# A two-level Strassen kernel: all attention chunks first, and x operands that stay in SBUF

## The chip, the cores and the metric

The kernel runs on one core of a Trainium2 chip. A core has TensorE (PE: matrix products, with the weight load shown apart as PEld), VectorE (DVE), ScalarE (ACT), GpSimd (POOL), SyncE (SP, which here issues nearly all DMAs) and 16 DMA engines; each engine runs its own instruction stream in order. The metric is the device time of one execution in microseconds (us), lower is better. Before the change it is 1186.68 us, the median of three runs (1186.55 to 1187.57).

## The reference

Two blocks follow each other. The first is a decayed linear attention with batch B=4, H=8 heads, S=768 positions and head width D=64; the second sends its output, seen as x of 3072 tokens by 512 features, through four experts.

```python
# attention, block by block along the sequence
intra = einsum('bhic,bhjc->bhij', qb, kb) * Dmask
intra = einsum('bhij,bhjd->bhid', intra, vb)
inter = einsum('bhid,bhde->bhie', qb * lam_pow, kv_state)
out[:, :, sl] = intra + inter
kv_state = lam_block * kv_state + einsum('bhsd,bhse->bhde', kb * rev_pow, vb)
# experts, E=4, DM=512, F=1024
p = domain_probs / (domain_probs.sum(-1, keepdims=True) + 1e-09)
for e in range(E):
    h = maximum(x @ w1[e], 0.0)
    out += p[:, e:e+1] * (h @ w2[e])
```

All data is fp32.

## The kernel before, in words

**Attention.** The work is cut into 24 chunks of 128 positions, six to a batch. A chunk has three pieces. `turn` transposes q and k on TensorE against an identity (L529), eight transposes, copies both from PSUM with ScalarE (L534, L535), scales q on VectorE (`qs`), and lets GpSimd multiply k by its decay (`decayed`). `scores` makes the key-query products into two PSUM banks (L551), and VectorE multiplies them by the decay mask into two tiles `st`. `values` reads the state (L574), multiplies masks and values (L579), and makes the next state's share (L587) in the unused half of one of its two banks; ScalarE copies the output (L592) into `xT`, and VectorE updates `kv`. In batches 2 and 3, from the third chunk on, q and k come in another way: `bring_across` lays them out again in DRAM in small pieces, and `turn_across` transposes 32 by 32 blocks on VectorE, so that TensorE has no transposes for these eight chunks.

**The experts.** Tokens are taken in three groups of 1024 (eight chunks), experts one after the other: units (g, e), 12 in all. Each unit has a first product x @ w1 and a second h @ w2. Both are written with Strassen's scheme in the Winograd form: seven outer products M1 to M7 of sums of quarters. The first product is split a second time: each outer M has seven inner products of two matmuls of 128 x 128 by 128 x 256 (`first_product`, L843), for which the seven inner operands of x and of w1 are loaded from DRAM, 896 KB each (`feed`). Evacuation is an add on VectorE (`tt`, recorded at L95), or a ScalarE copy (L851). The last group's second product is nested too (`nested_product`, L1123), with the last results turned at the end.

Operands are prepared on GpSimd: `prepare_w1`, `prepare_w2` and `prepare_x` form the quarter sums and inner sums and store them to DRAM (`w1_ops`, `w2_sums`, `x_ops`). They are lists of small steps called chores. `pump` issues them by a clock of slots `now`, an estimate `busy` of GpSimd's work (one slot for each 480 elements a partition), and puts a store two slots behind its work. `until` forces chores out where a load needs them. VectorE sums that may be delayed stand in the list `background`, from which `rest` takes one at a time; `soon` puts new items at its front.

**The order.** The first group's eight chunks are written out in ten iterations: iteration i has turn i, scores i-1 and values i-2, with three pairs of PSUM banks used in turn (`pairs[n % 3]`), so that turn i+1 takes the pair of values i-2. From iteration 4 quarters of unit (0,0)'s first products stand between the pieces. That unit alone uses one Strassen level (`direct_product`, L1253): each outer product is 16 matmuls from plain quarters of w1. The operands of unit (0,1) are formed on the fly (`own_x`, `own_w1`) and stored for later. From then on a loop runs over the units: it interleaves the second product of one unit with the first product of the next, seven steps of eight slots, and places one attention piece of the next group now and then in a slot.

`load` issues q, k and v of a chunk on SP as rows of 64 numbers. The pool of 128 x 512 tiles (`small`) has `NPOOL` = 47 buffers; `stream` has two buffers each for x and w1 operands.

Of the kernel before, what the change touches and what calls it, by code (L numbers as in the profile page):

```python
# [11 lines left out]
AF = mybir.ActivationFunctionType  # L12
# [5 lines left out]
NPOOL = 47  # L18
AHEAD = 2
# [3 lines left out]
def kernel(  # L23
# [11 lines left out]

# [22 lines left out]
    stream = ctx.enter_context(tc.tile_pool(name="stream", bufs=2))  # L76
    opool = ctx.enter_context(tc.tile_pool(name="o", bufs=CPG))
# [4 lines left out]

# [25 lines left out]

    nat = {}

    def load(n, names="qkv"):

        b, c = divmod(n, NCH)
        for name in names:
            x = small(f"{name}n")
# [12 lines left out]
    x_ops = dram.tile([NG, 7, P, 7, 256], FP32, name="x_ops")  # L128
# [4 lines left out]
    X_AT = {n: i for i, n in enumerate(("M1", "M7", "M6", "M4", "M5", "M2", "M3"))}  # L133


# [58 lines left out]

    def inner_x(eng, g, m, blk):
        at = {"B11": (0, 0), "B12": (0, 1), "B21": (1, 0), "B22": (1, 1)}
        inner(eng, ("x", g, m), x_ops[g, MS.index(m)], blk, T_OPS, at)
# [103 lines left out]
    xT = consts.tile([P, 4, G], FP32, name="xT")  # L301

    b11, b21 = xT[:, 0:2, 0:W], xT[:, 2:4, 0:W]
    b12, b22 = xT[:, 0:2, W:G], xT[:, 2:4, W:G]

    def prepare_x(g):

        st = {}

        def total(name, a, b, op):  # L310
            t = stage.tile([P, 2, W], FP32, name="xo", tag="st")
            halves(t[:], a, b, op)
            st[name] = t[:]

        def ready(m, blk):
            inner_x(nc.gpsimd, g, m, blk)

        return [lambda: ready("M1", b11), lambda: ready("M2", b21)], [
            lambda: total("T1", b12, b11, ALU.subtract), lambda: ready("M5", st["T1"]),
            lambda: total("T2", b22, st["T1"], ALU.subtract), lambda: ready("M6", st["T2"]),  # L320
            lambda: total("T3", b22, b12, ALU.subtract), lambda: ready("M7", st["T3"]),
            lambda: ready("M3", b22),
            lambda: total("T4", b21, st["T2"], ALU.subtract), lambda: ready("M4", st["T4"]),
        ]


# [3 lines left out]
    w1_now = {0: {}, 1: {}}  # L330

    def raw_w1(e, name):
        i, j = int(name[1]) - 1, int(name[2]) - 1
        if name in ("A21", "A22"):
            to = tuple(small("w1b")[:] for _ in range(2))
        else:
            t = stage.tile([P, 2, W], FP32, name="w1b", tag="st")
            to = t[:, 0], t[:, 1]
# [1179 lines left out]
```

## Time and profile before

| what | value |
|---|---|
| median of three runs | 1186.68 us |
| span of the profiled execution, first to last instruction | 1183.3 us |
| what lies around the span, median less span | 3.4 us |
| PE busy | 1175.7 us (99%), 6559 instructions |
| DVE busy | 790.7 us (67%) |
| POOL busy | 628.7 us (53%) |
| ACT busy | 274.0 us (23%) |
| moved by DMA | 324.23 MB, mean 274 GB/s |
| x operand loads | 70 of 896 KB, 6.4 us from issue to landing |
| w1 operand loads | 70 of 896 KB, 8.7 us from issue to landing |

The profile is of one execution; no total time of its own is given for it beyond the span, so the 3.4 us are the difference to the median of the runs. Busy shares are averages over the stages: the opening (attention of the first group with the first unit's direct products, up to about 90 us), the steady stage up to about 690 us, the last group with its nested second products, and the end. Matmuls overlap, each shown with its whole latency of 380 ns or so; how fast TensorE goes is read from the distance between their starts. A line such as L95 is a helper: the tiles' names tell the operations apart.

### The profile page before, as it was taken

The page shows a single profiled execution, that of the slowest core. Times are in us where ns is not written, and L with a number is a line of the kernel's source. Part 1 is how long each engine was busy: PE and PEld are TensorE (multiplying, and loading weights), DVE is VectorE, ACT ScalarE, POOL GpSimd, SP SyncE. Part 2 cuts the span into 40 slices and gives each one's busy share as a digit, 9 for nine tenths or more (in the row PEclk, how much of TensorE's full clock was granted, in tenths as well). Part 3 has the DMA queues.
Part 4 walks back from the last instruction along what each step waited for, and adds up shares of the span by engine and source line. Part 5 has one row for each costly group of instructions (what it writes and reads, how often), then busy time and mean ns, then how long its engine had stood idle before and what let it go on. Part 6 is the DMA issues. An engine that isn't in the chain of part 4 may idle for free.

```text
span 1183.3 us, 17880 instructions
## 1 busy us (share of the span) xinstructions
PE 1175.7 (99%) x6559; PEld 1022.7 (86%) x6559; DVE 790.7 (67%) x1333; ACT 274.0 (23%) x500; POOL 628.7 (53%) x600
## 2 busy tenths in 40 slices
PE   9999999999999999999999999999999999999998
PEld 8888888888888888888888888888888888888887
DVE  6785785567468857647856774773665676777785
ACT  3332122112211201211220120121243342341331
POOL 2756258349457900055244655416584693783884
PEclk9999999999999999999999999999999999999999
DMA  9797799999999997899998989998986657566543
GB/s 232 194 292 238 250 300 310 362 326 333 353 359 334 328 291 227 262 287 303 303 317 247 295 287 318 275 312 294 316 289 238 261 196 272 212 237 248 213 155 95
DMA packets 265608, 324.23 MB, mean 274 GB/s; under 512 B 121489, under 2 KB 206897, under 8 KB 265521
## 3 DMA queue, kind: packets, MB, share of 16 engines
q1 hardware_dynamic: 254912, 320.27, 81.6%
q10 hardware_dynamic: 10608, 2.82, 1.1%
q8 instruction: 52, 0.85, 0.3%
q14 instruction: 36, 0.29, 0.1%
HBM read 237.69 MB, written 89.54 MB: 277 GB/s over the span
## 4 chain that ended last, share of the span: by engine, by line
PE 94%; DVE 3%; DMA 2%; issue 0%; POOL 0%; SPq 0%; ACT 0%; DVEq 0%
PE pg L843 38%; PE q L897 32%; PE pq L1123 13%; PE pM L1253 2%; PE op L579 2%; PE sp L551 2%; PE pc L1253 2%; DMA w_ops<-ops 2%; PE op L574 1%; PE op L587 1%; DVE sums L95 0%; PE qp L529 0%; PE kp L529 0%; PE pg L1123 0%; DVE acc L95 0%; DVE m L95 0%
## 5 line engine op out<-in xcount | busy, mean ns | idle before, releaser
L843 PE MATMUL pg<-xs_in,ws_in 128*128 128x256 f32 x1960 | 469.8, 380 | 0.9 <-DVE m L95 0.9
L843 PEld LDWEIGHTS pg<-xs_in,ws_in 128*128 128x128 f32 x1960 | 371.2, 190 | 52.9 <-DVE m L95 2.3
L95 DVE TENSOR_TENSOR m<-pg,m 128x512 f32<-128x512 f32 x451 | 308.1, 687 | 106.5 <-PE pg L843 99.6
L897 PE MATMUL q<-w2t,hS 128*128 128x256 f32 x1024 | 243.4, 380 | 0.0
L897 PEld LDWEIGHTS q<-w2t,hS 128*128 128x128 f32 x1024 | 193.2, 190 | 27.0 <-issue 0.2
L913 DVE SCALAR_TENSOR_TENSOR acc<-q,gate,acc 128x256 f32<-128x256 f32 x192 | 92.5, 482 | 170.2 <-PE q L897 170.0
L897 PE MATMUL q<-w2t,m 128*128 128x256 f32 x768 | 182.7, 381 | 0.0
L897 PEld LDWEIGHTS q<-w2t,m 128*128 128x128 f32 x768 | 144.8, 190 | 20.5 <-issue 0.3
L855 ACT ACTIVATE m<-m 128x512 f32<-128x512 f32 x132 | 83.0, 630 | 283.6 <-DVE m L95 276.6
L95 POOL TENSOR_TENSOR m<-m,xT 128x512 f32<-128x512 f32 x64 | 80.7, 1276 | 71.6 <-ACT m L855 53.9
L95 POOL TENSOR_TENSOR kn<-kn,s_decay 128x512 f32<-128x512 f32 x20 | 22.5, 1126 | 140.7 <-PE kp L529 134.8
L95 DVE TENSOR_TENSOR sums<-pq,sums 128x256 f32<-128x256 f32 x153 | 64.2, 422 | 46.0 <-PE pq L1123 38.8
L851 ACT COPY m<-pg 128x512 f32<-128x512 f32 x88 | 51.6, 586 | 174.3 <-PE pg L843 173.4
L1123 PE MATMUL pq<-acc,w2t 128*128 128x256 f32 x352 | 86.6, 379 | 0.0
L95 POOL TENSOR_TENSOR ops<-w2b 128x256 f32<-128x256 f32 x24 | 17.9, 766 | 119.4 <-DMA w2b<-in_moe_w_dram 111.3
L1123 PEld LDWEIGHTS pq<-acc,w2t 128*128 128x128 f32 x352 | 66.8, 190 | 9.3 <-issue 0.3
L95 POOL TENSOR_TENSOR acc<-hT,hT 128x512 f32<-128x512 f32 x32 | 40.3, 1274 | 30.3 <-PE pq L1123 28.4
L95 POOL TENSOR_TENSOR w2o<-w2b 128x512 f32<-128x512 f32 x32 | 40.6, 1291 | 23.3 <-DMA w2b<-in_moe_w_dram 23.3
L786 ACT ACTIVATE m<-m 128x512 f32<-128x512 f32 x44 | 27.7, 630 | 101.8 <-DVE m L95 101.8
L95 DVE TENSOR_TENSOR hS<-m,m 128x512 f32<-128x512 f32 x56 | 45.3, 812 | 4.9 <-ACT m L855 4.9
L95 DVE TENSOR_TENSOR m<-m,m 128x512 f32<-128x512 f32 x56 | 47.2, 844 | 0.0
L95 POOL TENSOR_TENSOR acc<-hT,acc 128x512 f32<-128x512 f32 x32 | 40.7, 1273 | 7.4 <-PE pq L1123 5.4
(158 smaller groups left out, 1360.4 us busy)
## 6 DMA issues: line engine op xcount, KB each, us to landing
xs_in<-x_ops SPq DMA_DIRECT2D x70, 896.0 KB, 6.4
ws_in<-w_ops SPq DMA_DIRECT2D x70, 896.0 KB, 8.7
w2t<-w_ops SPq DMA_DIRECT2D x66, 256.0 KB, 6.8
w2t<-w_sums SPq DMA_DIRECT2D x64, 256.0 KB, 3.9
w_ops<-ops SPq DMA_DIRECT2D x28, 512.0 KB, 5.5
w2t<-in_moe_w_dram SPq DMA_DIRECT2D x48, 256.0 KB, 3.4
w2b<-in_moe_w_dram SPq DMA_DIRECT2D x32, 256.0 KB, 5.9
w_sums<-w2o SPq DMA_DIRECT2D x16, 512.0 KB, 5.1
```

The source lines that it names most:

```text
L95: eng.tensor_tensor(out=o, in0=a, in1=b, op=op)
L551: nc.tensor.matmul(out=sp[r][:, ac * C:(ac + 1) * C], lhsT=hc(kT)[half[r], ac], rhs=hc(qT)[half[r], ac], start=True, stop=True,)
L574: nc.tensor.matmul(out=op[r][half[x], a * C:(a + 1) * C], lhsT=kv[half[r], 2 * a + x], rhs=hc(qs)[half[r], 2 * a + x], start=(a == 0), sto ...
L579: nc.tensor.matmul(out=op[r][half[x], a * C:(a + 1) * C], lhsT=vn[:, 4 * r + 2 * a + x], rhs=hc(st[r])[:, 2 * a + x], start=(first and a = ...
L786: nc.scalar.activation(out=o[:], in_=o[:], func=AF.Relu)
L843: nc.tensor.matmul(out=p[:, j * 256:(j + 1) * 256], lhsT=ws[i][:, j * P:(j + 1) * P], rhs=xs[i], start=(fresh and j == 0), stop=True, skip ...
L851: nc.scalar.copy(out=new[at][:], in_=p[:])
L855: nc.scalar.activation(out=new[at][:], in_=new[at][:], func=AF.Relu)
L897: nc.tensor.matmul(out=p[:, s * DH:(s + 1) * DH], lhsT=h[A_OF[m]][:, c * 256 + s * P:c * 256 + (s + 1) * P], rhs=fed2[g, e, m][uu][:, c], ...
L913: nc.vector.scalar_tensor_tensor(out=o, in0=x, scalar=w, in1=o, op0=ALU.mult, op1=ALU.add)
L1123: nc.tensor.matmul(out=p[:, 0:256], lhsT=fed3[e, m, x // 2][:, x % 2, c * P:(c + 1) * P], rhs=b[B_OF[i]][:, c * 256:(c + 1) * 256], start= ...
L1253: nc.tensor.matmul(out=p[:, s * 256:(s + 1) * 256], lhsT=a[c][:, f:f + P], rhs=b[:, c, j * 256:(j + 1) * 256], start=(s == 0 and c == 0 an ...
```

## The change

- All 24 attention chunks stand at the start. Iterations 0 to 13 of the same three-piece pattern run with nothing between (`DENSE = 14`); scores come ahead of turn in iteration 3 alone. The remaining 33 pieces are spread over the first 35 slots of unit (0,0)'s first product, at a rate of `len(attention) / 35` a slot.
- All chunks are turned on TensorE; `bring_across`, `turn_across` and what belongs to them go.
- Unit (0,0) takes `first_product` with two Strassen levels like all others, with w1 operands formed on the fly in the stream buffers (`own_fill`, `own_inner`), and stored for later groups. `direct_product`, `own_x`, `own_w1` and the one-level sums go. Unit (0,1) reads its w1 operands from DRAM, as prepared by `prepare_w1(1)`.
- Seven tiles `xs` (pool `xp`, one buffer each) hold all inner operands of a group's x for its four units. Group 0's are written directly: values copies the plain quarters a second time, VectorE makes the quarter sums (`pair_sums`, chunks 4 to 7), and `x_inner` makes the inner sums, M1's and M2's on VectorE, the others on GpSimd.
- For groups 1 and 2, plain quarters and GpSimd's pair sums are stored in `x_blocks` (128 KB a piece), and `x_fill` brings 512 KB a block into a slot while the last unit of the group before runs; GpSimd then makes the inner sums. The stores and the 896 KB loads of `x_ops` are gone.
- While the dense part lasts, delayed VectorE work is issued at once; afterwards it goes through the front of `background`, and values forces what it needs (`settle_up`).
- `NPOOL` is 37; k and v are loaded into the buffers of `acc` and `w2`. The w2 operands of the last unit go to the seven x slots.

```diff
-NPOOL = 47
-AHEAD = 2
+NPOOL = 37
+DENSE = 14
...
+    xp = ctx.enter_context(tc.tile_pool(name="xp", bufs=1))
...
+    def x_inner(g, m, eng):
+        t = slots[g, m]
+        for o, x, y in ((4, 3, 1), (1, 1, 0), (5, 3, 1), (6, 2, 5)):
+            tt(eng, t[:, o], t[:, x], t[:, y], ALU.subtract)
+        made.add(("x", g, m))
+
+    def x_fill(g, m):
+        t = slot(g, m)
+        nc.sync.dma_start(out=whole(t), in_=x_blocks[g - 1, MS.index(m)])
+        chores.insert(0, lambda: x_inner(g, m, nc.gpsimd))
...
+        work = [once(f) for f in work]
+        owed[what] = work
+        if dense[0]:
+            settle_up(what)
+        else:
+            background[0:0] = work
...
     def values(n, tags):
+        settle_up(("qs", n), ("st", n), ("kv", n - 1))
...
+            nc.scalar.copy(out=x[:, r * 256:(r + 1) * 256], in_=op[r][:, 0:256])
+            if r in plain and g == 0:
+                nc.scalar.copy(
+                    out=whole(slots[0, plain[r]])[:, :, at], in_=op[r][:, 0:256].rearrange("p (a t) -> p a t", t=C),
+                )
...
+            for t, a, b in (("T1", b12, b11), ("T2", b22, o["T1"]), ("T3", b22, b12), ("T4", b21, o["T2"])):
+                tt(nc.vector if g == 0 else nc.gpsimd, o[t], a, b, ALU.subtract)
...
+    attention = [
+        (i, f, i - lag) for i in range(NT + 2)
+        for f, lag in (((scores, 1), (turn, 0), (values, 2)) if i == 3 else ((turn, 0), (scores, 1), (values, 2)))
+        if 0 <= i - lag < NT
+    ]
+
+    def attend():
+        i, f, n = attention.pop(0)
+        f(n, pairs[n % 3])
+        if not attention or attention[0][0] != i:
+            if i + 4 < NT:
+                load(i + 4, "qk")
+            if 4 <= i + 3 < NT:
+                load(i + 3, "v")
+        return i
...
+    chores.extend((
+        lambda: (own_fill("M1"), raw_w1("A21", "A22")), pause(4),
+        lambda: own_inner("M1"), lambda: own_sum("S1"), lambda: (own_fill("M5"), raw_w1("A11")),
+        lambda: own_inner("M5"), lambda: own_sum("S2"),
+        *prepare_w2(0),
+    ))
+    for i in range(DENSE):
+        while attention[0][0] == i:
+            at_turn = attention[0][1] is turn
+            attend()
...
+    rate = len(attention) / 35
+    for i, m in enumerate(SEQ):
...
+        for f in first_product(0, 0, m, blocks, ("g1", "g3")):
+            f()
+            now[0] += 1
+            rest()
+            pump()
+            credit += rate
+            while credit >= 1 and attention:
+                credit -= 1
+                attend()
...
-                if steps and (at > 0 or i > 1) and (x == 5 or (x == 2 and i in (1, 3, 5) and at not in (0, 3))):
-                    steps.pop(0)()
+                if x == 3 and i > 0 and g < LAST and ahead == (g, E - 1):
+                    x_fill(g + 1, SEQ[i - 1])
```

## The prediction

> **What bounds the kernel now.** I read the totals first, then the timeline of a late stretch, then the busy time by stage, then the opening 90 us in the chain of waits and the timeline, because the change rebuilds the opening.
>
> From the page's totals, a steady stretch of the timeline, and the stage table (columns: stretch; its length; busy time and instruction count of PE, PEld, DVE, ACT, POOL; clock; DMA share; GB/s):
>
> ```profile
> span 1183.3 us, 17880 instructions
> PE 1175.7 (99%) x6559; PEld 1022.7 (86%) x6559; DVE 790.7 (67%) x1333; ACT 274.0 (23%) x500; POOL 628.7 (53%) x600
> ...
> 703.90 1.89 PE L897 MATMUL q<-w2t,m 128*128 128x256 f32 x8
> 705.63 1.89 PE L843 MATMUL pg<-xs_in,ws_in 128*128 128x256 f32 x8
> ...
> 5.00:35.00 30.00, 29.06 (x352) 25.38 (x353) 20.41 (x40) 12.49 (x25) 5.39 (x5) 1.00 1.05 255
> 90.00:690.00 600.00, 598.85 (x3495) 518.25 (x3494) 405.94 (x662) 107.70 (x193) 294.19 (x305) 1.00 0.92 300
> ```
>
> TensorE never rests: 1.15 us idle in the 600 us of the steady stage. Eight matmul instructions start every 1.73 us, so one of 256 columns costs 0.216 us (each fp32 matmul of the program is two of them). The DMA engines are 92% busy there, but TensorE does not wait for them. All its waits named on the page of waits sum to about 4 us. So time can only come from fewer TensorE instructions or from those few us, and can be lost wherever TensorE is made to wait.
>
> One attention chunk from the opening, in the chain in order of time (start, duration, what), and the end of the chunk before it in the timeline:
>
> ```profile
> 20.23 0.44 PE qp L529 x4
> 20.66 0.44 PE kp L529 x4
> 21.10 1.09 PE sp L551 x16
> 22.19 0.60 PE op L574 x16
> 22.79 1.02 PE op L579 x16
> 23.81 0.46 PE op L587 x16
> 24.28 3.65 PE pM L1253 x16
> ...
> 17.67 0.37 ACT L592 COPY xT<-op 128x256 f32<-128x256 f32 x1 [0.78 <-PE op L579]
> 17.67 0.63 PE L587 MATMUL op<-vn,kn 128*64 128x64 f32 x16
> 18.23 1.99 PE L1253 MATMUL pM<-xT,w1b 128*128 128x256 f32 x8
> 18.35 0.37 ACT L592 COPY xT<-op 128x256 f32<-128x256 f32 x1 [0.31 <-PE op L587]
> 18.76 0.42 DVE L95 TENSOR_TENSOR kv<-kv,op 128x256 f32<-128x256 f32 x1 [0.52 <-ACT xT L592]
> ```
>
> A chunk is 4.05 us of TensorE (20.23 to 24.28): turn 0.88, scores 1.09, values 2.08. After its values the bank pair stays taken until VectorE has added the state, 19.18, while TensorE was through at 18.3. Today quarters of direct products (L1253) fill that time.
>
> The VectorE rows that matter, from the groups:
>
> ```profile
> L95 DVE TENSOR_TENSOR m<-pg,m 128x512 f32<-128x512 f32 x451 | 308.1, 687 | 106.5 <-PE pg L843 99.6 <-ACT m L851 0.7
> L95 DVE TENSOR_TENSOR st<-sp,s_decay 128x512 f32<-128x512 f32 x48 | 31.7, 680 | 3.2 <-PE sp L551 3.2
> L95 DVE TENSOR_TENSOR qs<-qT,q_decay 128x512 f32<-128x512 f32 x12 | 11.3, 938 | 3.5 <-ACT qT L534 3.4
> ```
>
> **What the Trainium skill says.** "Perfetto Trace Analysis", Identifying the Most-Contended Engine: matmul busy share is no measure of headroom since matmuls are pipelined; hence the spacing of starts above, which agrees (380 ns each, 216 apart). "PSUM — Partial Sum Buffer", PSUM bank collisions raise a hardware error: ScalarE and VectorE may not read one bank at once and must be ordered. The trace agrees: the state's add begins at 18.76, 0.04 after the second ScalarE copy (18.35 + 0.37), though its matmuls were done at 18.30. "SBUF — State Buffer", SBUF: two separate sides: VectorE with two SBUF inputs and GpSimd exclude each other for a whole instruction. It agrees: a qs product took 1.47 us at 16.44 while GpSimd worked on kn, against 0.69 alone. "DMA: Bandwidth & Descriptors", Specifications: 512 bytes or more for full rate. It agrees: q, k, v in 256-byte rows give 255 GB/s at a full share; the mixed traffic of 65 to 70 us gave 362.
>
> **The change, part by part.**
>
> *TensorE work.* Unit (0,0) goes from 7 x 16 = 112 matmuls to 7 x 7 x 2 = 98: 28 instructions fewer, 28 x 0.216 = -6.0 us. Eight chunks that came turned over DRAM are now turned on TensorE: 8 x 0.88 = +7.0. Chunks 8 to 11 lose the switches between attention and products (0.1 to 0.15 us each, two a chunk): -1. Sum 0.
>
> *x operands in SBUF.* 70 loads of 896 KB and the stores of x operands go; 14 fills of 512 KB and many 128 KB stores come. Worth nothing: the steady stage idles 1.15 us, and the three waits of products there (0.5 us at most each) are for VectorE, not DMA. GpSimd's x work moves but stays (four subtractions per block, 7 blocks, 2 groups); cover is GpSimd's 306 free us out of 600. A fill is queued on SP behind the end of the product that frees its slot, six steps of 13 us before its next use, so weights queued behind it lose little. With cover gone: 3.2 us a block.
>
> *Dense attention, iterations 4 to 13.* They need 10 x 4.05 = 40.5 us from 18.3, so 58.8. But the turn of iteration i+1 uses the bank pair of values (i-2), just issued, with no quarter between. Scores come first only in iteration 3. For group 0 ScalarE has an extra copy from the same bank (0.37), so the add runs 19.13 to 19.55 on the scale above; the four q transposes fit before it (18.23 to 18.67), the k transposes wait until 19.6: 0.96 us per iteration. For group 1, no extra copy: 0.56. VectorE keeps that pace: 0.94 + 2 x 0.68 + 0.62 + 0.42 = 3.3 us, 5.4 with the four new pair sums of chunks 4 to 7 (some 0.5 each).
> The DMA queue is the second limit. In queue order, q, k, v at 240 GB/s (786 KB, 3.3 us a chunk), weights and stores at 330 (w1 quarter 1.6, operand store 2.8): start at 2, four chunks 15.2, qk4 17.4, three w1 quarters, qk5 24.4; then M1's store and A11 delay qk8 to 38.7, two w2 blocks and M5's store qk10 to 51.3, two more blocks qk13 to 64.4. The iterations then end: 4 at 23.3; 5 at 28.0 (24.4 + 3.61 after k lands); 33.0; 38.0; 43.0; 48.0; 10 at 54.9 (51.3 + 3.61); 59.5; 64.1; 68.7. Loss 68.7 - 58.8 = +10. Bounds: +4 if the banks come free at once (DMA alone), +16 if the queue is 10% slower.
>
> *Interleaved attention, 33 pieces over 35 slots of the first product.* A slot issues one inner product (4 x 0.216 = 0.86 us), gives VectorE its add (0.69), takes one item of background and then one attention piece. New items go to the front, and four arrive per three slots; so the second mask of chunk n is always forced at values(n). Queue of VectorE then: the slot's add starts 0.2 after its matmuls, 0.69; a mask 0.68; the forced mask 0.68: ready 2.25 us after the slot's matmuls. TensorE reaches that operand after 0.60 + 0.26 = 0.9: a wait of 1.4. Likewise the turn after values: add 0.69, decay 0.45, state add 0.42 behind a slot of 0.86 + four transposes 0.44: again 1.4. Where the slot's result is a ScalarE copy (4 of 7 in M1 and M5) neither occurs. Slot by slot: values 15, 17 to 22 wait 1.4, values 16 0.65; turns 18, 19, 22, 23 1.4, turns 15, 16, 21 0.95, 0.55, 0.95. Sum 7 x 1.4 + 0.65 + 4 x 1.4 + 2.45 = 18.5. Bounds: 0 (VectorE ahead) to 30 (GpSimd's locks double the SBUF operations).
>
> *Rest of the first unit.* With attention used up, about 21 slots remain: 18.1 us plus the last two values 4.2, 22 for TensorE. VectorE has 21 x 0.69 + 20 sums of 512 columns x 0.83 + masks 2 = 33. Of the 11 us lacking some are already in the waits above, so I take +6; bounds 0 (sums postponed) to 12.
>
> *First weights of unit (0,1)*: stored and reloaded (8.7 us from issue to landing today) while 8 slots of 0.86 run: +1, bounds 0 to 8. *Waits of before in its opening* go: -1.
>
> Sum: 0 + 10 + 18.5 + 6 + 1 - 1 = +34.5. On the span 1183.3 + 34.5 = 1217.8; the 3.4 us between the span and the median of the runs stay, so 1186.7 + 34.5 = 1221.
>
> **Rivals.** (1) VectorE runs ahead in the interleaved part, so only the dense part costs: 0 + 10 + 4 (rest of the unit) + 1 - 1 = +14, 1201. For it: 106 us idle in front of product adds. Against: in the opening VectorE already stands in the chain of waits. (2) Not slower: the bank pair comes free before the turn needs it. Then TensorE's work is equal, scores and masks hide in products as at 90 to 690 us, and the waits of before vanish: 1186.7 - 4 = 1183. It decides if an iteration of the dense part stays at 4.1 us; from 4.3 on the sign turns. Against it, the ordering at 18.76. (3) Worse: the second expert's w1 operands (GpSimd 7 x 3.2 + 8 x 1.35 = 33 us) come late behind pair sums and own weights, and TensorE waits for most of them: +34 + 25, 1246. For it: one GpSimd queue carries it all; against: it has some 105 us of work before them in over 150 us. That operand traffic still limits and its removal speeds matmuls up is excluded by the 0.216 us spacing in the busiest stretches.
>
> **How the numbers follow.** The forecast 0.57 (own range 1208 to 1238), rival 1 0.24, rival 2 0.07, rival 3 0.12. The range 1196 to 1242 takes in rival 1 and the upper bounds of the forecast, leaving out rival 2 and most of rival 3. 0.2%, 2.4 us, is about what a measurement can tell from no change. Faster 0.05, same 0.02, slower 0.93.
>
> **What would show it.** Dense part: k transposes that wait for VectorE's kv or for DMA, and an end of that part near 69 us. Interleaved: waits of op (L579 of before) for st, and of kp for kv, some 1.4 each. Rest: VectorE at its full time, products waiting for m. After that, TensorE without gaps, with less DMA. I am wrong if TensorE's idle time in the first 190 us is under 10 us, or if the added time lies in later stages.

## The result, and the profile after

The changed kernel takes **1251.8 us** (median of four runs, 1251.0 to 1253.6) against 1186.6 for the kernel before beside it: a ratio of **1.055, 95% interval 1.0535 to 1.0565**. The sign was right and the size not: 65 us more instead of 34.5, above the range of 1196 to 1242. The profiled execution has a span of 1251.8 us, 68.5 more than before. In every run here the time of the profiled execution is 1.8 us above its span, so of the 3.4 us between span and median of the kernel before some 1.6 probably come from a profiled execution that was faster than the median. The profile of the changed kernel is the slowest of its four runs (1253.6). So the spans differ by 3.3 us more than the medians, and the account below, taken from the profiles, is one of spans.

Totals and granted clock from the page, then the busy time by stage (columns as in the prediction: PE, PEld, DVE, ACT, POOL, clock, DMA share, GB/s):

```profile
span 1251.8 us, 17937 instructions
PE 1197.9 (96%) x6595; PEld 1036.8 (83%) x6595; DVE 784.3 (63%) x1330; ACT 286.7 (23%) x522; POOL 630.4 (50%) x628
...
PEclk9889989999999999999999999999999999999999
```

```profile
5.00:35.00 30.00, 21.74 (x274) 18.61 (x276) 15.45 (x34) 12.13 (x26) 14.08 (x15) 0.86 1.04 257
300.00:900.00 600.00, 600.00 (x2781) 527.87 (x2781) 374.93 (x608) 98.52 (x162) 224.29 (x251) 1.00 0.66 215
```

From 300 to 900 us TensorE has no idle time (0.9 us before), though DMA moves 215 GB/s instead of 300. Between 5 and 35 us it is idle for 8.3 of 30 us, where it was idle for 0.9, and its clock there was 0.86 on average: the profile shows the half clock in stretches of 3.4, 6.8 and 10.2 us in the first 225 us. The list of waits of PE (total, times, longest):

```profile
PE pg L817 <- DMA ws_in<-w_ops: 10.3, 1, 10.3
PE kp L500 <- DVE kv L76: 9.1, 11, 1.6
PE op L546 <- DVE st L76: 7.8, 6, 1.7
PE qp L500 <- DMA vn<-in_v_dram: 7.7, 1, 7.7
PE op L559 <- POOL kn L76: 5.3, 1, 5.3
PE pg L817 <- DVE m L76: 4.2, 6, 1.6
PE kp L500 <- DVE kv L581: 2.8, 3, 1.7
```

The forecast waits are there (kp for kv, op for st, up to 1.7 each), and so are three long single ones that it did not have: 10.3, 7.7 and 5.3 us. The chain of waits shows what the second of them leads to. These are the same pieces that took 0.44, 0.44, 1.09 and 0.60 before:

```profile
27.43 3.34 DMA vn<-in_v_dram
30.76 0.04 issue
30.80 1.11 PE qp L500 x4
31.91 1.00 PE kp L500 x4
32.92 2.01 PE sp L520 x16
34.93 1.06 PE op L546 x16
```

TensorE was idle from 23.1 to 30.8 and then ran at half the clock until 37.0. The Trainium skill ("TensorE: Matmul & The Clock Gate", Part 1) states that the clock halves after an idle window of about 3.4 us and returns after a busy window of the same length. This case agrees on the halving: the clock fell at 26.8, 3.7 us into the wait. The return took 6.2 us of work here. The half clock also came for 3.4 us each at 149.7, 170.2 and 183.8, where no single wait is over 1.7 us, so one long idle stretch is not its only occasion; the measurement decides.

The product group as a whole has its old latency (group of the page):

```profile
L817 PE MATMUL pg<-xs,ws_in 128*128 128x256 f32 x2352 | 572.1, 382 | 14.7 <-DMA ws_in<-w_ops 10.3
```

Nor are VectorE's operations slower than before (0.687, 0.680 and 0.938 there; groups by shape):

```profile
L76 DVE TENSOR_TENSOR m<-pg,m 128x512 f32<-128x512 f32 x492 | 336.8, 688 | 146.9 <-PE pg L817 137.8 <-POOL acc L76 1.6 <-DMA w_ops<-w1o 0.8
L76 DVE TENSOR_TENSOR st<-sp,s_decay 128x512 f32<-128x512 f32 x48 | 31.2, 682 | 10.3 <-PE sp L520 10.1
L76 DVE TENSOR_TENSOR qs<-qT,q_decay 128x512 f32<-128x512 f32 x20 | 17.2, 862 | 5.8 <-ACT qT L505 4.5 <-DMA kn<-in_k_dram 1.2
```

**Account by stage**, from the starts of the matmuls. The time without waits is that of the stage's instructions: the dense part by the prediction's own end of 58.8; the interleaved part 10 turns, 11 scores, 12 values (45.8), 128 product instructions at 0.216 (27.6) and some 3 for switches; then 68 instructions (14.7) and the first 60 of the next loop (13.0).

| stage of the changed kernel | lasts | without waits | lost | predicted |
|---|---|---|---|---|
| dense attention, to 86.5 | | 58.8 | 27.7 | 10 |
| interleaved, 86.5 to 184.5 | 98.1 | 76.5 | 21.6 | 18.5 |
| rest of unit (0,0)'s first product, to 208.3 | 23.8 | 14.7 | 9.1 | 6 |
| first 60 product instructions after it, to 234.2 | 25.9 | 13.0 | 12.9 | 1 |
| all later work | 1014.0 | 1013.8 | 0.2 | 0 |

The last row compares the 1014.0 us from 234.2 to the last matmul with the same work before (102.3 to 1179.8, 1077.5, less 63.7 for the 16 attention chunks that stood in it, with their switches and three short waits). The losses sum to 71.5; 68.5 less that is -3.0 for TensorE's work and the waits of before, forecast as -1. So the whole loss lies in the first 234 us.

### The profile page after: what moved, and what is told of

It is laid out like the page before. It is cut to its first block, busy times and chain, and to the rows that moved or that the text cites. A ratio compares the mean times of both kernels' runs of the same rounds, so it can differ in the third digit from the quotient of the medians.

```text
span 1251.8 us, 17937 instructions
## 1 busy us (share of the span) xinstructions
PE 1197.9 (96%) x6595; PEld 1036.8 (83%) x6595; DVE 784.3 (63%) x1330; ACT 286.7 (23%) x522; POOL 630.4 (50%) x628
## 3 DMA queue, kind: packets, MB, share of 16 engines
q1 hardware_dynamic: 221696, 251.06, 62.9%
q10 hardware_dynamic: 10608, 2.82, 1.0%
## 4 chain that ended last, share of the span: by engine, by line
PE 90%; DVE 3%; DMA 2%; SPq 2%; POOL 1%; issue 1%; ACT 0%; ACTq 0%; DVEq 0%; POOLq 0%
PE pg L817 40%; PE q L871 31%; PE pq L1097 12%; PE op L551 2%; PE sp L520 2%; SPq L111 1%; PE kp L500 1%; PE op L546 1%; DVE st L76 1%; PE op L559 1%; DVE kv L76 0%; DVE m L76 0%; DVE sums L76 0%; DMA w_sums<-w2o 0%; PE qp L500 0%
## 5 line engine op out<-in xcount | busy, mean ns | idle before, releaser
L817 PE MATMUL pg<-xs,ws_in 128*128 128x256 f32 x2352 | 572.1, 382 | 14.7 <-DMA ws_in<-w_ops 10.3
L817 PEld LDWEIGHTS pg<-xs,ws_in 128*128 128x128 f32 x2352 | 445.5, 191 | 81.9 <-issue 11.3
L76 DVE TENSOR_TENSOR m<-pg,m 128x512 f32<-128x512 f32 x492 | 336.8, 688 | 146.9 <-PE pg L817 137.8
L829 ACT ACTIVATE m<-m 128x512 f32<-128x512 f32 x144 | 90.7, 630 | 346.9 <-DVE m L76 346.7
L76 POOL TENSOR_TENSOR m<-m,s_decay 128x512 f32<-128x512 f32 x64 | 80.4, 1273 | 63.0 <-ACT m L829 47.6
L76 POOL TENSOR_TENSOR xs<-xs 128x256 f32<-128x256 f32 x76 | 58.0, 764 | 107.2 <-DMA xs<-x_blocks 95.9
L825 ACT COPY m<-pg 128x512 f32<-128x512 f32 x96 | 56.2, 585 | 212.3 <-PE pg L817 192.2
L76 DVE TENSOR_TENSOR sums<-pq,sums 128x256 f32<-128x256 f32 x153 | 64.2, 422 | 46.0 <-PE pq L1097 35.8
L760 ACT ACTIVATE m<-m 128x512 f32<-128x512 f32 x48 | 30.3, 630 | 130.9 <-DVE m L76 130.9
L76 DVE TENSOR_TENSOR hS<-m,m 128x512 f32<-128x512 f32 x64 | 50.3, 786 | 15.4 <-ACT m L829 15.3
L76 POOL TENSOR_TENSOR acc<-hT,hT 128x512 f32<-128x512 f32 x32 | 40.3, 1272 | 30.1 <-PE pq L1097 28.2
L76 DVE TENSOR_TENSOR m<-m,m 128x512 f32<-128x512 f32 x64 | 53.6, 841 | 0.0
```

What stands on the lines that cost most here:

```text
L76: eng.tensor_tensor(out=o, in0=a, in1=b, op=op)
L760: nc.scalar.activation(out=o[:], in_=o[:], func=AF.Relu)
L817: nc.tensor.matmul(out=p[:, j * 256:(j + 1) * 256], lhsT=ws[i][:, j * P:(j + 1) * P], rhs=xs[i], start=(fresh and j == 0), stop=True, skip ...
L825: nc.scalar.copy(out=new[at][:], in_=p[:])
L829: nc.scalar.activation(out=new[at][:], in_=new[at][:], func=AF.Relu)
```

## The experiments

Where no other base is named, each starts from the changed kernel. Ratios are to the kernel before, run beside them; a ratio's 95% interval is about 0.0015 to 0.0031 to each side, some 2 to 4 us. "Interleaved" and "rest" are the stages of the account. The stages are read from one profile each. Nine of these kernels have the same instructions on every engine up to the end of the dense part (the changed kernel, a3, a6, a10, a12, a14, a15, a16 and a18), and they end it between 84.4 and 88.9; a difference of two or three us in that column can be chance.

| run | median us | ratio [95%] | dense ends | interleaved | rest |
|---|---|---|---|---|---|
| changed kernel | 1251.8 | 1.0550 [1.0535, 1.0565] | 86.5 | 98.1 | 23.8 |
| a3_sums_at_once | 1233.8 | 1.0403 [1.0385, 1.0420] | 86.5 | 77.6 | 23.6 |
| a1_gpsimd_sum | 1250.3 | 1.0541 [1.0525, 1.0556] | 83.7 | 97.9 | 24.1 |
| a2_scores_first | 1252.0 | 1.0557 [1.0541, 1.0573] | 90.1 | 92.6 | 24.4 |
| a5_w2_later | 1248.2 | 1.0521 [1.0505, 1.0536] | 79.9 | 98.1 | 26.9 |
| a7_kept_busy | 1258.3 | 1.0601 [1.0585, 1.0617] | 90.7 | 99.7 | 25.6 |
| a9_kept_busy_half | 1253.7 | 1.0568 [1.0537, 1.0599] | 85.7 | 96.3 | 24.5 |
| a6_clock_of_slots | 1243.8 | 1.0485 [1.0469, 1.0501] | 88.9 | 100.7 | 24.6 |
| a10_sums_and_clock | 1235.9 | 1.0418 [1.0399, 1.0437] | 85.3 | 86.7 | 26.7 |
| a12_spread | 1246.8 | 1.0508 [1.0492, 1.0523] | 86.1 | 124.3 | 1.2 |
| a8_all | 1234.8 | 1.0398 [1.0381, 1.0416] | 74.7 | 97.0 | 27.5 |
| a11_sums_w2_copy | 1230.8 | 1.0374 [1.0359, 1.0390] | 78.0 | 79.0 | 28.4 |
| a13_pair_sums_gpsimd | 1230.6 | 1.0374 [1.0358, 1.0390] | 74.6 | 80.9 | 28.2 |
| a14_no_unit_sums | 1229.9 | 1.0367 [1.0350, 1.0385] | 85.4 | 77.1 | 20.5 |
| a15_pair_sums_last | 1237.7 | 1.0425 [1.0409, 1.0440] | 86.7 | 78.5 | 22.7 |
| a16_stores_by_gpsimd | 1246.5 | 1.0497 [1.0474, 1.0520] | 84.4 | 81.0 | 22.2 |
| a17_best_stores_gpsimd | 1238.0 | 1.0429 [1.0411, 1.0447] | 77.0 | 83.1 | 33.6 |
| a18_last_sums_vector | 1233.7 | 1.0396 [1.0379, 1.0414] | 86.4 | 77.3 | 29.8 |

### TensorE's work alone: eight chunks turned on TensorE in the kernel before

```diff
-    ACROSS = {2: 2, 3: 2}
+    ACROSS = {}
...
+        if b not in ACROSS:
+            return
         c = ACROSS[b]
```

> The kernel before, with all chunks turned on TensorE and nothing laid out again in DRAM. Theory: 8 turns of 0.88 us are added to a TensorE that is never idle: +7.0 us, 1193.7. Rival (the freed VectorE transposes and DMA pieces pay for part of it): +0 to +3.

1192.4 us, ratio 1.0052 [1.0037, 1.0067]: +6.3, the forecast term of 7.0 inside its interval (4.4 to 7.9). This tests the turns alone, not the 28 instructions that go. TensorE's work is not where 31 us are missing.

### The interleaved part: sums of an operand at once

```diff
-        if dense[0]:
+        if True:
             settle_up(what)
```

> The kernel after, with qs, masks and state updates issued at once in the interleaved part too, as in the dense part, and not one per slot from the front of the list. Theory (the forced second mask and the late state update make TensorE wait, not VectorE's load): the 6 waits of values for st, 7.8 us, and some 3 us of the turn's waits go: 8 to 13 us faster, about 1241. Rival (VectorE has too much work there, whatever its order): unchanged within 3 us.

18.0 us less, more than expected, and the stage itself is 20.5 shorter. What is left of its waits (list of waits of PE of this kernel):

```profile
PE pg L817 <- DMA ws_in<-w_ops: 9.5, 1, 9.5
PE qp L500 <- DMA vn<-in_v_dram: 7.7, 1, 7.7
PE kp L500 <- DVE kv L76: 5.9, 8, 2.3
PE op L559 <- POOL kn L76: 5.3, 1, 5.3
```

The waits of op for st are gone, those of kp for kv are eight instead of eleven, and the half clock no longer occurs between 149 and 187 us. So the late second mask and the late state update cost near what the prediction said (18.5). But the 20.5 are more than their waits, of which the list names 15.0 in this stage: the half clock, on for 7.5 us of it, went together with them, and what it cost by itself was not separated. The three long waits stay.

### The opening: three blocks, one behind the other

The 7.7 us at 23.1 are listed for a load of v. The timeline of the changed kernel shows another engine held until the same moment (start, duration, idle before in brackets):

```profile
29.16 1.05 ACT L333 COPY ws_in<-w1o 128x1024 f32<-128x1024 f32 x1 [8.59 <-POOL w1o L76]
30.11 0.36 ACT L567 COPY xc<-op 128x256 f32<-128x256 f32 x1
30.80 0.71 PEld L500 LDWEIGHTS qp<-ident,qn 128*128 128x128 f32 x4 [7.82 <-ACT xs L569]
```

ScalarE's copy of the own weights' sum S1 waits 8.6 us for GpSimd, and behind it in the same stream stands the output copy that frees the bank pair. So a1 lets GpSimd make S1 a second time instead of the copy:

```diff
-            nc.scalar.copy(out=blk, in_=raw["S1"][:])
+            if a == "S1":
+                halves(blk, raw["A21"][:], raw["A22"][:], ALU.add)
+            else:
+                nc.scalar.copy(out=blk, in_=raw["S1"][:])
```

> The kernel after, with M5's w1 block summed on GpSimd instead of copied by ScalarE (the sum S1 is then made twice). Theory (ScalarE stands still behind that copy, which waits for GpSimd's S1, and the output copies of values behind it keep turn 5's banks): the wait of 7.7 us at 22.9 us shrinks to about 3.5, k of chunk 5 then being last at about 26.6, and TensorE's half clock after it shortens: 4 to 8 us faster than the kernel after, about 1246. Rival (DMA is what holds turn 5 anyway): unchanged, 1251 to 1252.

The wait fell to 3.3 and is then for q by DMA; turn 5 starts at 27.0 instead of 30.8, but turn 7 at 40.1 instead of 43.0 and the dense part ends only 2.8 earlier. The total is 1.5 less, within the intervals, as the rival has it. The cause of the wait is shown; the gain was given back behind it.

The 5.3 us are the second block. In the timeline, GpSimd:

```profile
68.02 8.43 SPq L231 DMA_DIRECT2D w_sums<-w2o  x2
73.42 2.67 POOL L76 TENSOR_TENSOR w2o<-w2b 128x512 f32<-128x512 f32 x2 [17.43 <-DMA w_sums<-w2o]
79.72 1.12 PE L559 MATMUL op<-vn,kn 128*64 128x64 f32 x16 [5.26 <-POOL kn L76]
```

A w2 sum waits 17.4 us for a staging buffer, whose store on SP begins only at 68.0, behind q, k and v; k's decay of the next chunk stands behind it on GpSimd. a5 prepares w2 of the first expert later, one product into the interleaved part:

```diff
         lambda: own_inner("M5"), lambda: own_sum("S2"),
-        *prepare_w2(0),
     ))
...
+            if i == 1:
+                chores.extend(prepare_w2(0))
```

> The kernel after, with the first expert's w2 sums prepared only from the second outer product on, not in the dense part. Theory (in the dense part SP's queue and the staging buffers carry too much: the sum T1 waits 17 us on GpSimd for the store of T3, which stands behind q, k, v on SP, and chunk 10's decayed k stands behind T1): the wait of 5.3 us of values at 74 us goes, the dense part ends near 78 instead of 86.5 us, and 6 to 10 us are won unless the sums then delay the w1 operands further. Rival (rate of q, k, v alone sets the dense part): it ends after 84 us, under 3 us faster.

The wait is gone and the dense part ends 6.6 earlier, as the theory has it; the rest of the unit takes 3 longer, so 3.6 remain, between theory and rival.

The prediction's bank wait is the third. a2 puts scores ahead of turn in every iteration:

```diff
-        for f, lag in (((scores, 1), (turn, 0), (values, 2)) if i == 3 else ((turn, 0), (scores, 1), (values, 2)))
+        for f, lag in ((scores, 1), (turn, 0), (values, 2))
```

> The kernel after, with scores ahead of turn in every iteration. Theory (turn i+1 waits for the bank pair of values i-2, until VectorE has added the state): the 14 waits of the k transposes for kv, 12 us together, lose about 1.1 us each, 8 to 12 us faster than the kernel after, about 1242. Rival (another engine's lag stands behind each of them, so that scores or values wait instead): less than 3 us faster, 1249 to 1252.

All kp waits for kv but one of 1.2 us vanish, and the time stays (the interval holds no change). The interleaved part is 5.5 shorter, the dense part 3.6 longer: op now waits 13.1 for GpSimd's kn once, and qp 9.7 for q and k by DMA. The rival was right. While loads and GpSimd come late, the bank wait stands in front of a later one, and taking it away brings the total nothing.

Last, the half clock. a7 puts dummy matmuls, no part of the result, before turn 5 and, in iteration 12, before the values of chunk 10, and a9 half as many (30 and 20):

```diff
+            if i == 5 and at_turn:
+                warm(60)
+            if i == 12 and attention[0][1] is values:
+                warm(40)
```

> The kernel after, with 60 dummy matmuls of 128 columns ahead of turn 5 and 40 ahead of values 10, where TensorE waits 7.7 and 5.3 us. Theory (a wait of some us halves TensorE's granted clock for the next 3 to 10 us, and that costs time by itself): the half clock at 27 to 37 and 78 to 85 us is gone, and the kernel is 2 to 6 us faster although it does more. Rival (TensorE waits for others in those stretches, so its clock costs nothing): 0 to 1 us, or slower by what the dummies overrun.

> The kernel after with half the dummies of the run before last (30 ahead of turn 5, 20 ahead of values 10), since each dummy proved to be two instructions and 60 of them lasted past the wait. Theory (a wait halves TensorE's clock, and the half clock costs time): they end inside the waits, the half clock at 27 to 37 and 78 to 85 us is gone, the dense part ends at 81 to 84 instead of 86.5 us, and the kernel is 2 to 5 us faster. Rival (TensorE's clock is worth nothing where DMA is behind anyway): the dense part ends at 86 to 87.

a7 settles nothing: its dummies outlast the waits (turn 5 at 37.8). In a9 the half clock at 27 to 37 and 78 to 85 is gone and turn 6 starts at 36.4 instead of 38.1; turn 7 starts at 42.9 instead of 43.0. The gain was given back within one iteration. To what, the chain of waits of a9 shows, and then ScalarE's timeline:

```profile
35.73 5.23 DMA w1b<-in_moe_w_dram
40.96 0.02 issue
40.98 0.40 ACTq L1142
```

```profile
41.48 0.58 ACT L505 COPY qT<-qp 128x512 f32<-128x512 f32 x1 [4.51 <-PE op L559]
```

ScalarE itself issues the small load of the domain probabilities (L1142). It does so only when a w1 load has landed, at 40.96, stands still for 4.0 us before that, and behind it in its stream stand the copies of turn 6's q and k and then the output copies that turn 7 waits for. In a1 it is idle for 5.0 us at the same place. This is a block of its own, and no run moves it. So a9 shows that removing these two stretches of half clock brings the total nothing here; it does not show what they cost where nothing behind them is late.

### What holds the dense part after that

a11 has the edits of a3, a1 and a5 together, and leaves the order of the pieces:

> The kernel after with VectorE's items at once, M5's block made by GpSimd, and the w2 sums after the dense part; the clock of slots as it was. Theory (dense part 86.5 to about 77, of which some 3 us are given back later as with the w2 sums alone): 1224 to 1229. Rival (the losses of the dense part only move to the wait for the first w1 operand): 1231 to 1234.

With both blocks gone k of chunk 13 lands at 65.0 (forecast 64.4; 69.8 in the changed kernel), and yet the part ends at 78.0, not 69. a13 takes group 0's pair sums off VectorE:

```diff
-                tt(nc.vector if g == 0 else nc.gpsimd, o[t], a, b, ALU.subtract)
+                tt(nc.gpsimd, o[t], a, b, ALU.subtract)
```

> The changed kernel with the S1 copy on VectorE, the sums of an operand issued at once, the w2 preparation at the start of the interleaved part, and the pair sums of group 0 on GpSimd instead of VectorE; beside a11_sums_w2_copy (1230.8, dense part to 78.0) it differs in the pair sums alone. Theory that VectorE (20.9 of 23 us busy between 55 and 78) sets the second half of the dense part: about 5 us of work leave it there, so the dense part ends at 72 to 74 and the time is 1225 to 1228. Rival that the q, k, v loads set it (k of chunk 13 lands at 64.2): end 77 to 79, time 1230 to 1233.

(S1 is made again by GpSimd, as in a1; the text on record names VectorE by mistake, and its 64.2 is before all of k has landed.) The stage table, a11 and then a13:

```profile
55.00:78.00 23.00, 17.65 (x290) 14.45 (x286) 20.90 (x34) 7.84 (x18) 15.20 (x18) 1.00 0.96 223
```

```profile
55.00:78.00 23.00, 19.33 (x285) 16.23 (x284) 16.34 (x26) 8.86 (x19) 21.98 (x26) 1.00 0.95 220
```

VectorE has 4.6 us less in this stretch, and the part ends 3.4 earlier; GpSimd is now busy for 22 of 23 us. But a17 below has the same dense part and ends it at 77.0, only 1.0 earlier than a11. Both profiles agree on iterations 9 to 11: from the start of turn 9 to that of turn 12 it is 17.3 us in a11, 14.8 in a13 and 15.0 in a17. So VectorE did hold these iterations, by some 2.4 us, and later ones gave part of it back. The total is the same (1230.6 to 1230.8), as the rival has it.

What stays on VectorE are the inner sums of M1 and M2, four to a block. The timelines of VectorE and TensorE in a13:

```profile
59.03 3.55 DVE L76 TENSOR_TENSOR xs<-xs 128x256 f32<-128x256 f32 x4
```

```profile
65.97 0.66 PE L503 MATMUL kp<-ident,kn 128*128 128x128 f32 x4 [2.38 <-DVE kv L76]
```

They stand ahead of qs, the masks and the state's add, VectorE has hardly a pause from 58.7 to 65.9, and k's transposes of turn 12 wait 2.4 for that add (2.6 in a17). No run moves these sums.

### The first w1 operand of unit (0,1), and the rest of the unit

The changed kernel's chain from the last attention values to the first product of unit (0,1), parts of it:

```profile
188.92 4.49 DMA ws_in<-in_moe_w_dram
...
197.82 1.22 POOL to L76
...
202.58 0.53 SPq L607
...
206.33 4.85 DMA w2t<-in_moe_w_dram
211.18 0.02 issue
211.19 4.46 DMA w_ops<-w1b
...
215.78 5.14 DMA ws_in<-w_ops
220.92 0.14 issue
221.06 3.75 PE pg L817 x8
```

There is no VectorE in this chain: load of own weights, GpSimd's pair sums (`to`), their stores on SP (L607), the w2 load behind them, the store of the operand, and only then its load back. The clock of chores `now` is not moved on by attention pieces. a6 moves it on:

```diff
                 credit -= 1
                 attend()
+                now[0] += 1
+                pump()
```

> The kernel after, with the clock of slots advanced once more for each attention piece placed in the first product, so that the list of GpSimd's chores is issued twice as fast there. Theory (GpSimd starves, 8 of 20 us busy at 120 to 180 us, because chores are paced by slots that now last 2.7 us; the operands of unit (0,1) therefore come late): the wait of 10.3 us for the first w1 operand falls below 3 us, 7 to 12 us faster, 1240 to 1245. Rival (GpSimd's work or its waits for buffers, not its pace, make it late): under 3 us faster.

The first 60 product instructions then take 13.0 us, the time without waits, instead of 25.9: this is the lost 12.9, wait and half clock together. 8.0 of it reach the total, as the theory has it; the interleaved part is 2.6 slower, and the dense part, with the same instructions, 2.4 in this profile. With a3 added it is another matter:

> The kernel after with VectorE's items at once and the faster clock of slots. Theory (the two losses are in different places, 18 and 8 us, and add up): 1224 to 1228. Rival (as in the run with all edits, GpSimd's chores issued earlier hold up chunks or w1 operands that attention needs): above 1231.

1235.9, no better than a3 alone and on the rival's side: a new wait of 6.3 for an own-weights load stands at 134.9, and the rest grew. Nor does spreading the attention over all slots (`/ 35` to `/ 54` on top) help:

> The kernel after with VectorE's items at once, the faster clock of slots, and attention spread over 54 of the first product's 56 slots instead of 35. Theory (after the last attention piece VectorE, not TensorE, sets the pace of the first product, some 10 us lost, and attention pieces would hide it): the first product ends without such a tail, 5 to 10 us faster than the same two edits without it, 1216 to 1222. Rival (the tail is GpSimd's w1 operands, M3 and M4 above all): within 3 us of them, or slower, since the pair sums and with them the operands of unit (0,1) come later.

The theory is wrong by 25 us; slower is what the rival allowed. From 187.9 on a product waits 10.3 for VectorE's m, and attention now runs to the end of the unit. The edits of a1, a2, a3 and a6 together, with w2 prepared at the start of the interleaved part, show the same pattern:

> The kernel after with all edits together: GpSimd makes M5's block, scores first in every iteration, VectorE's items at once, w2 sums after the dense part, faster clock of slots. Theory (the named waits are the whole loss, TensorE's work being that of before): 1190 to 1205; what remains is the rate of q, k, v in the dense part and VectorE in the rest of the first unit. Rival (contention of DMA and VectorE in the new opening, whatever the order): above 1220, as a3 alone gave 1233.8.

1234.8, as the rival has it, with a dense part that ends 11.8 earlier, and waits of 7.2 for kn and 9.3 for own weights in the interleaved part.

Four runs on top of a3 try single links of the chain. a14 leaves out the 16 sums for unit (0,0)'s second product; a15 queues the pair sums of later groups last; a16 issues their stores from GpSimd; a18 puts the last 16 of these sums on VectorE:

```diff
 # a14
+        if key[:2] == (0, 0):
+            h["S3"], h["S1"], h["S2"], h["S4"] = h["A11"], h["A22"], h["A12"], h["A12"]
+            del h["A21"]
+            return
 # a15
-            chores.insert(0, sums)
+            chores.append(sums)
 # a16 (a17: the same on a13)
-                store(lambda: [nc.sync.dma_start(out=x_blocks[g - 1, MS.index(m), :, :, at], in_=o[t])
-                               for m, t in B_OF.items() if t in o])
+                for m, t in B_OF.items():
+                    if t in o:
+                        nc.gpsimd.dma_start(out=x_blocks[g - 1, MS.index(m), :, :, at], in_=o[t])
 # a18
-                tt(nc.vector if g == 0 else nc.gpsimd, o[t], a, b, ALU.subtract)
+                tt(nc.vector if g == 0 or n >= 20 else nc.gpsimd, o[t], a, b, ALU.subtract)
```

> The changed kernel with the sums issued at once and without the 16 sums of operands for the second product of unit (0,0): plain halves stand in for S1 to S4, so that part of the output is another; beside a3_sums_at_once (1233.8, rest of the first unit 23.6 us) it leaves 16 VectorE sums of some 0.83 us out. Theory of the prediction that VectorE sets the rest of the first unit: rest 15 to 18 us, time 1225 to 1228. Rival that the chain of GpSimd's inner sums, the own weights' load and the stores and loads behind it sets the rest: 22 to 24 us and 1232 to 1235.

Between the two: the rest is 20.5, 3.1 less, for some 13 us of VectorE work. Of the 8.9 us that a3 loses in this stage, 3.1 go with these sums, and 2.5 are a wait for w2t. In the changed kernel itself every wait of TensorE named in this stage is for VectorE's m, 4.2 in all, and VectorE (the third busy time) is busy for most of it:

```profile
184.50:208.30 23.80, 19.30 (x74) 12.78 (x71) 20.46 (x32) 7.20 (x13) 21.67 (x23) 0.94 0.58 191
```

So VectorE does set much of this stage there, and the chain above sets the wait that follows it. In a14 the first w1 operand keeps TensorE waiting 10.0.

> The changed kernel with the sums issued at once, and the pair sums of groups 1 and 2 queued behind the other preparation on GpSimd instead of ahead of it; beside a3_sums_at_once (1233.8, where the wait for the first w1 operand of unit (0,1) is 9.5 and the rest of the first unit 23.6). Theory that the pair sums standing ahead on GpSimd make the operands of the own weights, w2 and the second expert's w1 late: the wait for the w1 operand falls under 2 us, the rest to about 17, the time to 1218 to 1224. Rival that another item of the same queue takes their place: some operand still comes 5 us or more late and the time is 1230 or more.

The rival is right: the w1 wait falls to 3.8, another wait of 6.2 appears in the same loop at 214, and the total is 3.9 worse.

> The changed kernel with the sums of an operand issued at once and the stores of the pair sums of groups 1 and 2 issued by GpSimd, right behind the sums, instead of by SP; beside a3_sums_at_once (1233.8) it differs in the queue of these stores. Theory that the tail of the first unit is held by SP's order (in a3 the last pair sums' stores at 167.6 and 182.0 stand ahead of the load of own weights at 168.1 and of the w2t load at 185.7): the rest of the first unit falls from 23.6 to 16 to 19 us, the wait for w2t (2.5) goes, the time is 1226 to 1230. Rival that GpSimd's own work sets it: rest 22 to 25 us and 1232 to 1235.

Wrong for both, by more than 11 us. In GpSimd's timeline of this kernel each group of four stores now takes the engine itself:

```profile
187.22 2.82 POOL L609 DMA_DIRECT2D x_blocks<-to  x4 [0.29 <-POOL to L76]
...
194.04 2.82 POOL L609 DMA_DIRECT2D x_blocks<-to  x4 [0.30 <-POOL to L76]
...
196.34 1.95 POOL L76 TENSOR_TENSOR ops<-w1b 128x256 f32<-128x256 f32 x2
```

That is 0.70 us a store. The w2 wait (2.5 in a3) is gone, so SP's order did hold that load. But the four groups of stores in the tail add 11.3 us ahead of the first w1 operand, and its wait is 18.7 instead of 9.5: what is put into GpSimd's stream there arrives nearly whole.

> The kernel of a13_pair_sums_gpsimd (1230.6; w2t wait 5.1, w1 operand wait 7.3, first unit to 183.7) with the stores of the pair sums of groups 1 and 2 issued by GpSimd instead of SP. Theory of SP's order: the w2t wait falls under 2 us, the first unit ends at 174 to 178, the time is 1221 to 1226. Rival: the second expert's first w1 block, loaded only at 174.1 because its buffer still held w2 work, keeps its place, so that its wait grows by what the first unit gains: wait of 10 or more and 1229 to 1232.

The same on a13: 7.4 worse, w2 wait 6.6, w1 wait 7.0. Both expectations missed it.

> The changed kernel with the sums of an operand issued at once and the 16 pair sums of the last four chunks (20 to 23) on VectorE instead of GpSimd; beside a3_sums_at_once (1233.8, w1 operand wait 9.5, first unit to 187.7) it differs in the engine of these 16 sums. Theory that GpSimd's order after the last values (16 pair sums of 0.73 to 1.24 us around the own weights' sums, 164.7 to 185.3) makes the first w1 operand late: its wait falls by 7 to 8 us to about 2, the time to 1224 to 1228. Rival that VectorE, now with 16 more sums of some 0.7 us, holds the rest of the first unit instead: the first unit ends at 193 or later and the time is 1231 or more.

The w1 wait falls to 2.6, as the theory has it, and the unit ends at 193.5 instead of 187.7, as the rival has it; the total stays. The timeline of GpSimd and then that of SP in this kernel:

```profile
180.38 4.47 POOL L76 TENSOR_TENSOR ws_in<-ws_in 128x256 f32<-128x256 f32 x4 [21.92 <-DMA x_blocks<-to]
```

```profile
167.78 7.83 SPq L607 DMA_DIRECT2D x_blocks<-to  x12
175.71 0.55 SPq L336 DMA_DIRECT2D ws_in<-in_moe_w_dram  x1
```

GpSimd is idle for 21.9 us before the last own weights, because their load on SP (L336) stands behind twelve stores that now wait for VectorE's sums: it is issued at 175.7, in a3 at 168.1. Counted from the last values to the first product of unit (0,1), the chain takes 36.6 us in a3 (164.1 to 200.7) and 35.8 in a18 (163.7 to 199.5), by two different ways. No one engine is its bound: it is a load, sums, a store, a load in series, across GpSimd and SP, each in order. Which order would shorten it was not found. No version tried comes near the kernel before; the best two are at 1.0374.

## Why the prediction was wrong

**TensorE's work, sum 0:** right as far as tested. Eight turns measured +6.3 for +7.0 (b1); the -6.0 and the switches had no run of their own, and the account leaves -3.0 for all of this and the old waits, against -1.

**x operands in SBUF, worth nothing:** right. 69 MB less are moved, and all later work takes 1014.0 against 1013.8.

**Dense attention, +10:** wrong, 27.7. The bank wait and the load order in it are real: k of chunks 5 and 8 lands at 26.7 and 41.1 for 24.4 and 38.7. But the step costed TensorE, the banks, VectorE and the DMA queue, and let the own weights' and w2's preparation run for nothing beside them on ScalarE and GpSimd. Those stand in the same in-order streams as attention's copies and k's decay: a ScalarE copy held 8.6 us by GpSimd, and a GpSimd sum held 17.4 us by a store that SP issued behind q, k and v. In the changed kernel the 27.7 hold the two long waits (13.0), waits for kv of 5.5 and, by an estimate from 14.7 us of work at half clock, some 7 for that. With both blocks moved (a11) the end falls from 86.5 to 78.0.

The step also had VectorE keep pace, which its own numbers do not give: 5.4 us of VectorE in an iteration with pair sums do not fit into its iterations of 5.0. And it left out the inner sums of M1 and M2, which took 1.8 us a block in the changed kernel and 3.0 to 3.9 in a11, a13 and a17. Of the 9.3 still over the forecast in a11, taking the pair sums off VectorE gained some 2.4 in iterations 9 to 11, and at the end of the part 3.4 (a13) or 1.0 (a17). Of the 5.9 left in a13, the starts of the turns put 3.4 before turn 12 (62.9 for 59.5), carried on from iteration 5, where q came late and the half clock held until 33.7, and 2.2 in iteration 12, behind the inner sums. That is a reading of the trace, not tested. A queue 10% slower, the step's upper bound, is not what the landing times of a11 show: k is 3.3 late at chunk 5 (27.7) and 0.6 at chunk 13.

**Interleaved attention, +18.5:** right in mechanism; 21.6 were lost and 20.5 went with the two late items (a3). That the size is so near is in part luck: the waits named there sum to 15.0, and the half clock, which had no term, is part of what remains.

**Rest of the first unit, +6:** 9.1, inside its bounds and with the mechanism as forecast: products wait for m, and VectorE is busy for 20.5 of 23.8 us. The step took all 21 slots as products (18.1 us); but one slot in eight of an outer product has none, and 17 products (14.7 us) were left. How much of the 9.1 is VectorE's alone is open: 16 of its sums left out gained 3.1 (a14), in a kernel where a w2 load was late too.

**First weights of unit (0,1), +1, bounds 0 to 8:** wrong, 12.9. The step took the time from issue to landing and had the operand ready to store in time. The chores' order was the thing to follow: pair sums that the last values release go to the front of the queue, and the operand's sums, store and load come behind them. 10.3 us are the wait; the other 2.6 go with the half clock that came in the wait and outlasted it (a6 takes both away).

**Rivals.** Rival 3 has the nearest time (1246) and this mechanism, the second expert's w1 operands late behind pair sums and own weights, but it met only the first operand (12.9, for the 25 it gave to most of them); that its total is near is due to 17.7 us in the dense part that it did not have. Rival 1 (VectorE ahead in the interleaved part) fell with the st waits, rival 2 with the sign.

**The half clock** had no term. What it costs by itself no run separates: at the first w1 operand it went together with the wait (a6), in the interleaved part with the late items (a3), and in the dense part dummy matmuls that removed two stretches of it brought the total nothing (a9), with ScalarE held behind one of them.

**Why the pieces do not add.** The single gains of a3 (18.0), a6 (8.0), a5 (3.6) and a1 (1.5) make 31.1; four edits of this sort and a2 together gained 17.0 (a8). Each takes time from TensorE that GpSimd's, SP's and VectorE's queues still need, so the next wait moves up: a8, a10 and a12 each have new waits of 6 to 10 us. The forecast summed its terms as if each stood alone. So did the theories of the combinations: those of a8, a10 and a12 missed and their rivals held, a11 came between the two, and a17 missed both.

## What to carry to other kernels

When work is moved out from under long products, list for every engine what stands in its stream between two pieces of the moved work, and follow each item's own release, not only TensorE's and the queue with the most bytes: one copy or one store held in order holds all behind it. A preparation that hid under products for nothing has a price as soon as the products are gone. And measure stages, not only totals: several edits here gained 5 to 10 us in one stage and gave part or all of it back in the next.

## What the runs showed of the hardware

- After waits of TensorE of 5 to 10 us its clock was half for 3.4 to 13.7 us in all; in the changed kernel it came back 3.8 to 6.2 us after work had resumed. Dummy matmuls in the wait removed it (a9).
- It was also half for 3.4 us at a time where TensorE only had waits of up to 1.7 us (changed kernel, 149.7, 170.2 and 183.8), and not between 149 and 187 us once most of these waits were gone (a3).
- A 128 KB store issued from GpSimd took 0.70 us of GpSimd's own time (2.82 for four, a16).
- GpSimd's 256-column subtraction took 0.73 us alone and up to 1.24 beside VectorE's sums of two SBUF operands (a3, 177 to 183 us).
- A DMA that ScalarE issues started 0.02 us after the landing of another DMA, a load of w1, after 4.0 us without work (a9, 40.98): issuing a DMA can hold an engine's stream as a copy can.
